# First queries on SP and ScalarE, a third of pair 1's queries loaded alone, one x transposition moved: a BigBird attention and gMLP kernel

## The chip, the cores and the metric

The kernel runs on one core of a Trainium2 chip. The metric is the device time of one execution in microseconds (us), lower is better; the median of three runs of the kernel before is 214.83 us. The engines of the core are called here PE (TensorE, with its weight loads as PEld), DVE (VectorE), ACT (ScalarE), POOL (GpSimd) and SP (SyncE, which here issues DMAs and does nothing else).

## The reference

Batch 4, 8 heads, 768 positions, head dimension 64. First a block-sparse attention, then a gMLP layer over its output. Cut to what matters:

```python
scores = scale * np.matmul(q, k.transpose(0, 1, 3, 2))        # [4, 8, 768, 768]
mask = (|blk_i - blk_j| <= 1) | (blk_i in {0, 23}) | (blk_j in {0, 23})
mask[qb*32:(qb+1)*32, kb*32:(kb+1)*32] = True                 # 3 sampled kb for each of 24 qb
attn = softmax(np.where(mask, scores, -1e9))
x = matmul(attn, v)                                           # -> [4, 768, 512]
h = np.maximum(x @ w_in, 0.0)                                 # 512 -> 1024
u, v = h[..., :512], h[..., 512:]
v_n = (v - mean(v)) / sqrt(var(v) + 1e-6)
gated = u * (einsum('ts,bsd->btd', w_spatial, v_n) + b_spatial[None, :, None])
out = gated @ w_out                                           # [4, 768, 512], float32
```

The same 24 by 24 block mask serves all heads and batches.

## The kernel before, in words

**Pairs and heads.** Two heads make a pair; there are 16 pairs, four to a batch element. For a pair the kernel loads `k`, `q` and `v` in float32 (384 KB each, helper `load`, L103 to L107) into staging tiles `st_k`, `st_q`, `st_v`, of which each name has three buffers. It casts them to bf16 (`cast`, L115 to L134): `k` and `q` go side by side into a tile `nat` with positions on the partitions, `v` goes into `vv`. `nat` is then transposed, so that the head dimension is on the partitions, and copied into `kq`, one row of columns for each head: 768 columns of keys (`K_`) and then 768 of queries (`Q_`). For the first four pairs TensorE does the transpositions (`head` L278 for pair 0, `tr_first` and `tr_rest` L348 and L356 for the others) and VectorE the copies out of PSUM; later pairs are transposed by DMA.

**The mask.** Rows 64 to 87 of `kq` (`MR`) hold the mask: for keys a one-hot of the block, for queries the 24 allowances (0 or -300) of the query's block. The scores matmul contracts over 88 rows and so adds the mask. The key rows are made once for head 0 by iota and compare; the query rows come from three small matmuls (`mask_rows`, L272) whose results are copied by ACT (twice) and DVE (once). `rows` (L239) copies both kinds of rows from head 0 to the other heads, on ACT, POOL or DVE.

**Slots.** The main loop (L807) goes through slots. In slot s, in program order: the scores of the slot (`qk_unit`, four matmuls of 256 columns, or two of 512, L406, then one Exp over 128x1024 on ACT, L411), what is listed in `pre` for the slot, the attention-times-`vv` matmuls that are due (`av_unit`, L452; normalisation by L434 and L435), what is listed in `at` (`when`), some steps of the gMLP products from a queue (`run_queue`, L546), and what is listed in `late`. The first 36 slots treat batch element 0 in units of three slots: `UNITS` 0 and 1 are the two heads of pair 0, units 2, 3, 4 the first third of the queries of pairs 1, 2, 3, and so on. The order is written out by hand and each engine executes its instructions in the order of the program.

The entries that matter here: pair 1's first transpositions (`tr_first(1)`: all keys and the first third of the queries) in slot 4, `tr_first(2)` in slot 7, `tr_first(3)` in slot 10; the rest of the queries of pair 1 (`tr_rest(1)`) in slot 8. `av_unit` of unit 0 begins in slot 5 and needs pair 0's `v`; that of pair 2 begins in slot 12. `xtr_third(u)` transposes a finished third of the attention output `x` for the gMLP; those of units 1 and 2 stand in `late` of slot 13, unit 1's first (L715 and L716).

**Queues.** DMAs are issued by SP one after the other in program order, except for the first keys and first queries of head 0, which ACT issues (L137, L138). SP's order is: sampled blocks, the rest of head 0's and head 1's keys, head 1's queries, then `k1 q1 v0 k2 q2 v1 k3 q3 v2`, the last third of pair 0's queries, `v3`, eight pieces of `w_in`. A load waits on SP for a free staging buffer, and what follows on SP waits with it. Pair 0's queries keep their buffer until their last third has been loaded and cast (L320, L324), so that the load of pair 3's queries has the choice of the two buffers of pairs 1 and 2 alone. POOL makes nearly all of the casts, in the same order as the loads: `k1 q1 v0 k2 q2 v1 k3 q3`, a `rows` copy, `v2 v3`, the last of pair 0's queries, `w_in`.

**Fillers.** `filler(n, to)` issues matmuls of zeros that only keep TensorE busy: 26 at the start, and `FILL2 = (6, 0, 2)` at three places of the setup.

Of the kernel before, what the change touches and what calls it, by code (L numbers as in the profile page):

```python
# [10 lines left out]
FP32 = mybir.dt.float32  # L11
# [6 lines left out]
def _listify(ap: bass.AP) -> bass.AP:  # L18
    t = ap.tensor
    if isinstance(t.shape, tuple):  # L20
        t = dataclasses.replace(t, shape=list(t.shape))
        ap = dataclasses.replace(ap, tensor=t)
    return ap
# [3 lines left out]
def kernel(  # L27
# [16 lines left out]
    nc = tc.nc  # L44

    B, H, S, D = q.shape
# [3 lines left out]
    NCH = S // 128  # L50
# [12 lines left out]
    TC = NCH // NT  # L63
    TW = TC * 128
    S0 = NT * NG * 3
    FILL, FILL2, FILL3 = 26, (6, 0, 2), 4
    U_DVE = (0, 1, 2, 3)

    const = ctx.enter_context(tc.tile_pool(name="const", bufs=1))
# [1 line left out]
    psum = ctx.enter_context(tc.tile_pool(name="psum", bufs=1, space=bass.MemoryType.PSUM))  # L71
# [13 lines left out]
    MR = slice(D, KR)  # L85
    K_, Q_ = slice(0, S), slice(S, 2 * S)

    def qcols(t0, n=1):
        return slice(S + t0 * TW, S + (t0 + n) * TW)
# [4 lines left out]
    def dram(src, p, hs=slice(0, 2), cs=slice(0, NCH)):  # L94
        b, g = divmod(p, NG)
        return src[b, 2 * g + hs.start:2 * g + hs.stop].rearrange(
            "h (p c) d -> p h (c d)", c=NCH)[:, :, cs.start * D:cs.stop * D]

    H0, H1, BOTH = slice(0, 1), slice(1, 2), slice(0, 2)
    ALLC, C01, C03, C45 = slice(0, NCH), slice(0, TC), slice(0, 2 * TC), slice(2 * TC, NCH)  # L100
    SRC = {"k": k, "q": q, "v": v}

    def load(p, nm, hs=BOTH, cs=ALLC, eng=nc.sync):  # L103
        if (nm, p) not in st:
            st[nm, p] = work.tile([128, 2, S // 2], FP32, tag="st_" + nm, bufs=3, name="st_" + nm)
        eng.dma_start(out=st[nm, p][:, hs, cs.start * D:cs.stop * D],  # L106
                      in_=dram(SRC[nm], p, hs, cs))  # L107
# [4 lines left out]
    def nat0_view():  # L112
        return nat[0].rearrange("p c h d -> p (c h d)").rearrange("p (h x) -> p h x", h=2)

    def cast(p, nm, eng, hs=BOTH, cs=ALLC):  # L115
        if nm == "v":
            dst = vv[p % NVV][:, hs, cs, 0:D]
        else:
            if p not in nat:
                nat[p] = work.tile([128, 2 * NCH, 2, D], BF16, tag="nat", bufs=4, name="nat")  # L120
            c0 = 0 if nm == "k" else NCH
            dst = nat[p][:, c0 + cs.start:c0 + cs.stop].rearrange("p c h d -> p h c d")[:, hs]
        src = st[nm, p].rearrange("p h (c d) -> p h c d", d=D)[:, hs, cs]
        if p == 0 and nm != "v":
            dst = nat0_view()[:, hs, (c0 + cs.start) * D:(c0 + cs.stop) * D]
            if cs is not C45:
                dst = dst[:, 0].rearrange("p (i t d) -> p t i d", t=2, d=D)
                src = src[:, 0].rearrange("p (t i) d -> p t i d", t=2)
            else:
                dst = dst.rearrange("p h (c d) -> p h c d", d=D)  # L130
        if eng is nc.scalar:
            nc.scalar.activation(out=dst, in_=src, func=AF.Copy)
        else:
            eng.tensor_copy(out=dst, in_=src)  # L134

    samp = const.tile([KR, 2 * NR], I32)
    load(0, "k", H0, C03, eng=nc.scalar)  # L137
    load(0, "q", H0, C03, eng=nc.scalar)  # L138
    nc.sync.dma_start(out=samp[MR], in_=_listify(sampled_blocks).bitcast(I32))
    load(0, "k", H0, C45)  # L140
    load(0, "k", H1)
    load(0, "q", H1, C03)
    load(1, "k")
    load(1, "q")
    load(0, "v")
    load(2, "k")
    load(2, "q")
    load(1, "v")


# [27 lines left out]
    wps = psum.tile([128, 512], FP32, tag="av", bufs=2)  # L178

    def filler(n, to):  # L180
        for _ in range(n):
            nc.tensor.matmul(out=to[:, 0:128], lhsT=warm, rhs=warm, start=True, stop=True)
# [28 lines left out]
    PL, DV = nc.gpsimd, nc.vector  # L211
# [27 lines left out]
    def rows(hs, cs, eng=nc.vector):  # L239
        src = kq[MR, 0:1, cs].to_broadcast([NB, hs.stop - hs.start, cs.stop - cs.start])  # L240
        if eng is nc.scalar:
            nc.scalar.activation(out=kq[MR, hs, cs], in_=src, func=AF.Copy)
        else:
            eng.tensor_copy(out=kq[MR, hs, cs], in_=src)

    cast(0, "k", nc.scalar, H0, C03)
    rows(H1, K_, nc.scalar)
    rows(slice(2, 3), slice(0, 512), nc.scalar)
    cast(0, "q", PL, H0, C03)
    cast(0, "k", PL, H0, C45)  # L250
    cast(0, "k", PL, H1)
    cast(0, "q", PL, H1, C03)


# [2 lines left out]
    def moe_tag():  # L257
        moe_tags.rotate(1)
        if moe_tags[0] in held:
            moe_tags.rotate(1)  # L260
        return moe_tags[0]

    def bank(nm="ps", tag=None):
        return psum.tile([128, 1024], BF16, tag=tag or moe_tag(), bufs=2 if tag else 1, name=nm)
# [7 lines left out]
    def mask_rows(ps, t0, n, copy, rs=slice(0, KR)):  # L272
        nc.tensor.matmul(out=ps[:, 0:n * TW], lhsT=bm[rs],
                         rhs=kq[rs, 0, t0 * TW:(t0 + n) * TW], start=True, stop=True)
        return lambda: copy(kq[MR, 0, qcols(t0, n)], ps[0:NB, 0:n * TW])


    def head(ps, h, c0, n, at=0):  # L278
        for i in range(0, n, 2):
            nc.tensor.transpose(out=ps[:, at + i * 64:at + (i + 2) * 64],  # L280
                                in_=nat0_view()[:, h, (c0 + i) * D:(c0 + i + 2) * D],
                                identity=ident)

    def split0(ps, h, c0, n, t, copy=dve_copy):
        w = n * 64
        copy(kq[0:D, h, c0 * 128 + t * w:c0 * 128 + (t + 1) * w], ps[t * D:(t + 1) * D, 0:w])

    K4, K2, Q4 = (0, 2 * TC), (2 * TC, NCH - 2 * TC), (NCH, 2 * TC)
    ps0 = bank()
    head(ps0, 0, *K4)  # L290
    split0(ps0, 0, *K4, 0)
    split0(ps0, 0, *K4, 1)
    filler(FILL2[0], wps)
    psq = bank("psq", "av")
    head(psq, 0, *Q4)
    split0(psq, 0, *Q4, 0)
    filler(FILL2[1], wps)
    mask_rows(psum.tile([128, 1024], FP32, tag="sc", bufs=2, name="mq"), 0, 1, act_copy)()
    m1 = mask_rows(psum.tile([128, 512], FP32, tag=moe_tag(), bufs=1, name="mq"), 1, 1, act_copy)
    m2 = mask_rows(psum.tile([128, 1024], FP32, tag="sc", bufs=2, name="mq"), 2, 1, dve_copy, MR)  # L300
    filler(FILL2[2], wps)
    split0(psq, 0, *Q4, 1)
    m1()
    m2()
    rows(H1, qcols(0, NT), PL)
    rows(slice(2, 3), slice(512, S), PL)

    cast(1, "k", PL)
    cast(1, "q", PL)
    cast(0, "v", PL)  # L310
    load(3, "k")
    cast(2, "k", PL)
    cast(2, "q", PL)
    cast(1, "v", PL)
    load(3, "q")
    cast(3, "k", PL)
# [379 lines left out]
    at, late, pre = {}, {}, {}  # L696

    def when(slot, *fns):
        at.setdefault(slot, []).extend(fns)

    def c(f, *a, **kw):
        return lambda: f(*a, **kw)

    K_Q0 = slice(0, S + TW)
    ROWS = [(1, 2, 8, qcols(0)), (1, 3, 4, K_), (5, 4, 6, K_), (6, 6, 8, K_), (14, 4, 8, qcols(1, 2))]
    when(0, second)
    when(1, third)
    when(2, lambda: filler(FILL3, psum.tile([128, 512], FP32, tag=moe_tag(), bufs=1, name="wps")))
    for p, sl in ((1, 4), (2, 7), (3, 10)):
        when(sl, c(tr_first, p))  # L710
    for sl, h0, h1, cs in ROWS:
        when(sl, c(rows, slice(h0, h1), cs))
    for p, sl in ((1, 8), (2, 11), (3, 14), (0, 17)):
        when(sl, c(tr_rest, p, 2 if p == 0 else 1))
    for u in range(1, len(UNITS)):  # L715
        late.setdefault({1: 13, 2: 13}.get(u, 3 * u + 7), []).append(c(xtr_third, u))  # L716

    def moe_begin(b):
        moe[b] = Moe(b)
# [139 lines left out]
```

## Time and profile before

| | |
|---|---|
| median of three runs | 214.83 us (214.56 to 215.42) |
| profiled execution | 215.21 us, of which 213.4 us are the span from the first to the last instruction |
| busy share of the span | PE 97%, PEld 61%, DVE 62%, ACT 80%, POOL 34% |
| first Exp of the scores (slot 0) | starts at 6.02 us |
| the 36 Exps of batch element 0 (L411) | 6.02 to 44.03 us, with 2.4 us of idle time of ACT among them |
| DMA | 41.70 MB, mean 195 GB/s; 306 to 386 GB/s from 6 to 15 us |

Each row of a timeline gives the start, the duration, the engine, the line of the kernel, the operation with its output and input tiles, the number of merged instructions, and in brackets the idle time of the engine before it with what ended that time. Durations and starts are us from the start of the span. The scores of the first slots start on PE at 5.38, 5.94, 7.09, 8.10, 8.93 (slots 0 to 4), 10.93, 12.29, 13.58, 15.10, 16.14 (5 to 9), 16.84, 18.24, 19.18, 20.14 and 21.59 us (10 to 14).

From the DMA view, the landing times of the loads (issue plus time to landing): head 1's queries 5.57, `k1` 7.16, `q1` 9.87, `v0` 10.95, `k2` 12.0, `q2` 13.0, `v1` 14.1, `k3` 15.1, `q3` 16.2, `v2` 17.2, the last third of pair 0's queries 17.6, `v3` 18.7 us.

### The profile page before, as it was taken

The page shows a single profiled execution, that of the slowest core. Times are in us where ns is not written, and L with a number is a line of the kernel's source. Part 1 is how long each engine was busy: PE and PEld are TensorE (multiplying, and loading weights), DVE is VectorE, ACT ScalarE, POOL GpSimd, SP SyncE. Part 2 cuts the span into 40 slices and gives each one's busy share as a digit, 9 for nine tenths or more (in the row PEclk, how much of TensorE's full clock was granted, in tenths as well). Part 3 has the DMA queues.
Part 4 walks back from the last instruction along what each step waited for, and adds up shares of the span by engine and source line. Part 5 has one row for each costly group of instructions (what it writes and reads, how often), then busy time and mean ns, then how long its engine had stood idle before and what let it go on. Part 6 is the DMA issues. An engine that isn't in the chain of part 4 may idle for free.

```text
span 213.4 us, 5299 instructions
## 1 busy us (share of the span) xinstructions
PE 206.6 (97%) x2151; PEld 130.9 (61%) x2151; DVE 131.9 (62%) x287; ACT 171.0 (80%) x226; POOL 72.9 (34%) x119
## 2 busy tenths in 40 slices
PE   8799999999999999999999999999999999999992
PEld 7578887866666665665665565566656656544441
DVE  7589875988854535385887445286784433476551
ACT  6969999999999899979989788978989787266021
POOL 6589669867572405042442040130120000012000
PEclk9969999999999999999999999999999999999999
DMA  5999799999999999999691497697100324610265
GB/s 161 345 342 332 249 316 218 340 191 326 266 375 190 292 191 299 236 280 304 127 259 37 73 289 172 198 307 116 37 3 19 67 52 94 235 55 0 51 172 200
DMA packets 62780, 41.70 MB, mean 195 GB/s; under 512 B 44580, under 2 KB 57508, under 8 KB 62756
## 3 DMA queue, kind: packets, MB, share of 16 engines
q1 hardware_dynamic: 62324, 40.97, 74.7%
q10 hardware_dynamic: 432, 0.39, 0.6%
q8 instruction: 17, 0.28, 0.5%
q14 instruction: 7, 0.06, 0.1%
HBM read 24.38 MB, written 6.29 MB: 144 GB/s over the span
## 4 chain that ended last, share of the span: by engine, by line
PE 92%; DMA 3%; SPq 1%; ACT 1%; POOL 0%; DVE 0%; issue 0%; ACTq 0%
PE ps_moe L546 33%; PE ps L419 22%; PE ps_av L470 13%; PE ps_t L546 7%; PE ps L406 7%; PE ps_av L452 4%; PE ps_sc L546 4%; DMA st_q<-in_q_dram 3%; PE ps L267 1%; SPq L106 1%; PE ps_av L267 1%; ACT osb L217 0%; POOL nat L134 0%; ACT a_all L423 0%; DVE xn L435 0%
## 5 line engine op out<-in xcount | busy, mean ns | idle before, releaser
L423 ACT ACTIVATE a_all<-ps 128x768 bf16<-128x768 f32 x144 | 113.9, 812 | 14.9 <-PE ps L419 7.4
L419 PE MATMUL ps<-kq 88*128 88x384 bf16 x288 | 70.5, 325 | 0.1
L470 PEld LDWEIGHTS <-a_all 128*128 128x128 bf16 x864 | 46.5, 97 | 20.0
L470 PE MATMUL ps_av<-vv,a_all 128*128 128x65 bf16 x864 | 51.2, 194 | 0.0
L419 PEld LDWEIGHTS <-kq 88*128 88x128 bf16 x288 | 28.0, 98 | 31.0 <-issue 0.9
L546 PE MATMUL ps_moe<-w_in_t,xt 128*128 128x512 bf16 x144 | 44.0, 378 | 0.0
L411 ACT ACTIVATE a_all<-ps 128x1024 bf16<-128x1024 f32 x36 | 35.1, 1025 | 3.4 <-PE ps L406 2.9
L546 PE MATMUL ps_moe<-vn,w_spt 128*128 128x512 bf16 x108 | 32.7, 378 | 0.0
L134 POOL CAST nat<-st_k 128x768 bf16<-128x768 f32 (+2 forms) x17 | 13.6, 802 | 41.1 <-DMA st_k<-in_k_dram 40.8
L434 DVE RECIPROCAL rc<-ps_av 128x6 f32<-128x6 f32 (+1 forms) x36 | 6.7, 185 | 28.2 <-PE ps_av L470 26.6
L614 DVE SCALAR_TENSOR_TENSOR un<-ps_moe,b_col,un 128x512 bf16<-128x512 f32 x18 | 13.5, 750 | 16.7 <-PE ps_moe L546 16.1
L406 PE MATMUL ps<-kq 88*128 88x256 bf16 (+1 forms) x140 | 22.9, 286 | 0.7 <-ACT a_all L411 0.7
L583 POOL TENSOR_SCALAR std<-mv 128x3 f32<-128x3 f32 (+1 forms) x9 | 2.1, 238 | 62.2 <-DVE mv L580 45.5
L546 PE MATMUL ps_moe<-w_out_t,gt 128*128 128x512 bf16 x72 | 21.5, 378 | 0.0
L546 PEld LDWEIGHTS <-xt 128*128 128x128 bf16 x192 | 15.4, 97 | 7.2 <-DVE xt L214 0.2
L435 DVE TENSOR_TENSOR xn<-ps_av,rc 128x384 bf16<-128x384 f32 (+1 forms) x36 | 18.5, 513 | 1.2
L579 DVE BATCH_NORM_STATS2 stats<-vn 128x6 f32<-128x512 bf16 x24 | 16.5, 687 | 1.4 <-ACT vn L574 0.9
L134 POOL CAST nat<-st_q 128x768 bf16<-128x768 f32 (+1 forms) x18 | 14.1, 782 | 6.9 <-DMA st_q<-in_q_dram 6.5
L406 PEld LDWEIGHTS <-kq 88*128 88x128 bf16 x140 | 12.8, 100 | 4.6 <-issue 0.8
L134 POOL CAST vv<-st_v 128x768 bf16<-128x768 f32 x16 | 13.6, 855 | 5.7 <-DMA st_v<-in_v_dram 5.6
L452 PEld LDWEIGHTS <-a_all 128*128 128x128 bf16 x288 | 14.2, 100 | 2.0 <-issue 0.7
L214 DVE COPY kq<-tt 64x1536 bf16<-64x1536 bf16 x24 | 15.0, 627 | 0.3
(84 smaller groups left out, 211.8 us busy)
## 6 DMA issues: line engine op xcount, KB each, us to landing
st_v<-in_v_dram SPq DMA_DIRECT2D x16, 384.0 KB, 6.0
out_dram<-osb SPq DMA_DIRECT2D x23, 256.0 KB, 3.1
st_k<-in_k_dram SPq DMA_DIRECT2D x15, 384.0 KB, 4.4
st_q<-in_q_dram SPq DMA_DIRECT2D x15, 384.0 KB, 5.4
ws_f<-in_moe_w_spatial_dram SPq DMA_DIRECT2D x6, 384.0 KB, 6.6
w_f<-in_moe_w_in_dram SPq DMA_DIRECT2D x8, 256.0 KB, 5.9
w_f<-in_moe_w_out_dram SPq DMA_DIRECT2D x4, 256.0 KB, 4.2
st_q<-in_q_dram SPq DMA_DIRECT2D x2, 128.0 KB, 4.7
```

The source lines that it names most:

```text
L134: eng.tensor_copy(out=dst, in_=src)
L214: nc.vector.tensor_copy(out=o, in_=i)
L406: nc.tensor.matmul(out=ps[:, at:at + n * TW], lhsT=kq[:, h, ci * 128:(ci + 1) * 128], rhs=kq[:, h, qcols(t0, n)], start=True, stop=True)
L411: nc.scalar.activation(out=out, in_=ps, func=AF.Exp, scale=0.125)
L419: nc.tensor.matmul(out=ps[:, hf * 512:hf * 512 + HALF], lhsT=kq[:, j % H, ci * 128:(ci + 1) * 128], rhs=kq[:, j % H, S + hf * HALF:S + (hf ...
L423: nc.scalar.activation(out=a_ref["h", j][:, ci, :].rearrange("p (b c) -> p b c", b=2), in_=ps.rearrange("p (b c) -> p b c", b=2)[:, :, 0:H ...
L435: nc.vector.tensor_tensor(out=out, in0=ps[:, :, 0:D], in1=rc[:, 0:n].to_broadcast([128, n, D]), op=ALU.mult)
L452: nc.tensor.matmul(out=av_ref[u][:, to, :], lhsT=a_ref[u][:, at:at + 128], rhs=vv[pp % NVV][:, h, ci, :], start=(ci == 0), stop=(ci == NCH ...
L470: nc.tensor.matmul(out=av_ref[j][:, qc, :], lhsT=a_ref["h", j][:, ci, qc * 128:(qc + 1) * 128], rhs=vv[p % NVV][:, h, ci, :], start=(ci == ...
L546: nc.tensor.matmul(out=ref["ps"][:, 0:w], lhsT=lhs(i), rhs=rhs(i), start=(i == 0), stop=(i == n - 1))
L579: nc.vector.bn_stats(out=stats, in_=self.vn[:, tcc, :])
L614: nc.vector.scalar_tensor_tensor(out=self.un[:, tcc, :], in0=ps, scalar=b_col[:, tcc:tcc + 1], in1=self.un[:, tcc, :], op0=ALU.add, op1=AL ...
```

## The change

It does four things.

1. The first queries of head 0 are issued by SP, behind the sampled blocks, instead of by ACT, and are cast by ACT instead of POOL. ACT's copies of mask rows shrink (head 1's key rows in two halves, the second half behind the two copies of query rows) and head 2's key rows are made by DVE in slot 1 instead of by ACT and POOL. POOL casts head 1's keys before the rest of head 0's.
2. The setup's order changes: the three mask matmuls contract over the 24 mask rows alone, and the copies out of PSUM are in the order keys, queries, keys, queries. Four of the eight fillers of `FILL2` go.
3. Pair 1's queries are loaded and cast in two parts: the first third (`C01`, 128 KB, rows of 512 bytes) at the old place, the other two thirds (`C25`, 256 KB) behind pair 2's queries, on SP and on POOL.
4. `xtr_third(2)` moves from `late` of slot 13 to `pre` of slot 14, which is behind slot 14's scores.

```diff
-    FILL, FILL2, FILL3 = 26, (6, 0, 2), 4
+    FILL, FILL2, FILL3 = 26, (2, 2), 4
...
     load(0, "k", H0, C03, eng=nc.scalar)
-    load(0, "q", H0, C03, eng=nc.scalar)
     nc.sync.dma_start(out=samp[MR], in_=_listify(sampled_blocks).bitcast(I32))
+    load(0, "q", H0, C03)
     load(0, "k", H0, C45)
     load(0, "k", H1)
     load(0, "q", H1, C03)
     load(1, "k")
-    load(1, "q")
+    load(1, "q", cs=C01)
     load(0, "v")
     load(2, "k")
     load(2, "q")
+    load(1, "q", cs=C25)
     load(1, "v")
...
     cast(0, "k", nc.scalar, H0, C03)
-    rows(H1, K_, nc.scalar)
-    rows(slice(2, 3), slice(0, 512), nc.scalar)
-    cast(0, "q", PL, H0, C03)
+    cast(0, "q", nc.scalar, H0, C03)
+    rows(H1, slice(0, 384), nc.scalar)
+    cast(0, "k", PL, H1)
     cast(0, "k", PL, H0, C45)
-    cast(0, "k", PL, H1)
     cast(0, "q", PL, H1, C03)
...
     split0(ps0, 0, *K4, 0)
-    split0(ps0, 0, *K4, 1)
     filler(FILL2[0], wps)
     psq = bank("psq", "av")
     head(psq, 0, *Q4)
+    m0 = mask_rows(psum.tile([128, 1024], FP32, tag="sc", bufs=2, name="mq"), 0, 1, act_copy, MR)
+    m0()
     split0(psq, 0, *Q4, 0)
+    split0(ps0, 0, *K4, 1)
+    m1 = mask_rows(psum.tile([128, 512], FP32, tag=moe_tag(), bufs=1, name="mq"), 1, 1, act_copy, MR)
+    m1()
+    split0(psq, 0, *Q4, 1)
+    m2 = mask_rows(psum.tile([128, 1024], FP32, tag="sc", bufs=2, name="mq"), 2, 1, dve_copy, MR)
     filler(FILL2[1], wps)
-    mask_rows(psum.tile([128, 1024], FP32, tag="sc", bufs=2, name="mq"), 0, 1, act_copy)()
-    m1 = mask_rows(psum.tile([128, 512], FP32, tag=moe_tag(), bufs=1, name="mq"), 1, 1, act_copy)
-    m2 = mask_rows(psum.tile([128, 1024], FP32, tag="sc", bufs=2, name="mq"), 2, 1, dve_copy, MR)
-    filler(FILL2[2], wps)
-    split0(psq, 0, *Q4, 1)
-    m1()
     m2()
+    rows(H1, slice(384, S), nc.scalar)
     rows(H1, qcols(0, NT), PL)
-    rows(slice(2, 3), slice(512, S), PL)
 
     cast(1, "k", PL)
-    cast(1, "q", PL)
+    cast(1, "q", PL, cs=C01)
     cast(0, "v", PL)
     load(3, "k")
     cast(2, "k", PL)
     cast(2, "q", PL)
+    cast(1, "q", PL, cs=C25)
     cast(1, "v", PL)
     load(3, "q")
...
-    ROWS = [(1, 2, 8, qcols(0)), (1, 3, 4, K_), (5, 4, 6, K_), (6, 6, 8, K_), (14, 4, 8, qcols(1, 2))]
+    ROWS = [(1, 2, 8, qcols(0)), (1, 2, 4, K_), (5, 4, 6, K_), (6, 6, 8, K_), (14, 4, 8, qcols(1, 2))]
...
     for u in range(1, len(UNITS)):
-        late.setdefault({1: 13, 2: 13}.get(u, 3 * u + 7), []).append(c(xtr_third, u))
+        where, slot = (pre, 14) if u == 2 else (late, 13 if u == 1 else 3 * u + 7)
+        where.setdefault(slot, []).append(c(xtr_third, u))
```

More of the change, by code (lines that the diff above doesn't have):

```diff
@@ L99 @@
     H0, H1, BOTH = slice(0, 1), slice(1, 2), slice(0, 2)
-    ALLC, C01, C03, C45 = slice(0, NCH), slice(0, TC), slice(0, 2 * TC), slice(2 * TC, NCH)
+    ALLC, C01, C03 = slice(0, NCH), slice(0, TC), slice(0, 2 * TC)
+    C25, C45 = slice(TC, NCH), slice(2 * TC, NCH)
     SRC = {"k": k, "q": q, "v": v}
```

## The prediction

> **What bounds the kernel now.** I began with the page's rows of slices (where engines idle, where the clock falls), then the chain of waits over the first 23 us, the timeline there, and the waits of TensorE. From 21.5 us to the end the waits show none for PE: it is dense, in program order. A microsecond won or lost before 22 us is therefore passed on to the end nearly whole.
>
> The chain that ended last, in order of time (start, duration, what):
>
> ```profile
> 3.04 6.83 DMA st_q<-in_q_dram
> 9.92 0.84 POOL nat L134
> 10.80 0.29 PE ps L267 x2
> 11.09 0.85 PE ps L406 x2
> ...
> 20.98 0.43 DVE xn L435
> 21.42 0.05 issue
> 21.46 0.28 PE ps_av L267 x2
> 21.75 0.44 PE ps L406 x4
> ```
>
> Pair 1's queries are issued at 3.04, land at 9.87 and are cast by 10.75; only then can the last two transpositions of `tr_first(1)` run, and slot 5's scores behind them. Later the chain passes once more through a vector operation: `xtr_third(2)` waits for `xn`, with slot 14's scores queued behind it. The timeline around it, PE and ACT:
>
> ```profile
> 10.80 0.29 PE L267 MATMUL ps<-ident,nat 128*128 128x128 bf16 x2 [0.94 <-POOL nat L134]
> 11.98 1.02 ACT L411 ACTIVATE a_all<-ps 128x1024 bf16<-128x1024 f32 x1 [1.27 <-PE ps L406]
> 21.46 0.28 PE L267 MATMUL ps_av<-ident,xn 128*128 128x128 bf16 x2 [0.25 <-DVE xn L435]
> 22.23 18.74 ACT L411 ACTIVATE a_all<-ps 128x1024 bf16<-128x1024 f32 x19 [0.40 <-PE ps L406]
> ```
>
> Busy time in three stretches (PE first, PEclk behind POOL):
>
> ```profile
> 7.56:10.97 3.41, 2.05 (x22) 1.47 (x21) 1.44 (x5) 3.15 (x4) 1.39 (x2) 1.00 1.05 370
> 10.97:14.39 3.42, 3.42 (x28) 2.26 (x26) 3.19 (x4) 2.05 (x2) 2.82 (x4) 0.50 1.04 354
> ```
>
> A stretch with PE busy 2.05 of 3.41 us is followed by one at half clock; the stretch before it, with 3.09 busy, was not. What the half clock costs: the chain's five pieces of scores and attention of slots 5 to 7 (0.85, 0.53, 0.85, 0.44, 0.79) sum to 3.46, at full clock the same pieces are 0.44, 0.26, 0.44, 0.26, 0.44 = 1.84; so 1.62 us of PE time.
>
> The third view is SP's queue:
>
> ```profile
> 6.18 0.82 SPq L106 DMA_DIRECT2D st_k<-in_k_dram  x1
> 10.77 0.37 SPq L106 DMA_DIRECT2D st_q<-in_q_dram  x1
> ```
>
> `q3` is issued 0.02 us after the cast of `q1` ends (9.92 + 0.83 = 10.75): it waits for a buffer, and `v2`, the rest of pair 0's queries, `v3` and `w_in` wait behind it.
>
> **Part 1 and 2, the setup.** SP gets one more issue (0.43) ahead of everything; ACT loses one (0.46), which only lets its table load start earlier, and then it waits for keys that land at 0.72 + 2.2 = 2.92. The first queries landed at 1.15 + 2.5 = 3.65; from SP, issued at 1.21, I take 3.6. ACT's cast: 0.40, by the row of the keys (128x256, 0.40), so 4.0 against 4.13 on POOL. Then on ACT 0.49 of mask rows (24x384, between the 24x256 copy of 0.37 and the 24x512 copy of 0.61), two copies of 0.37, 0.49 again: 4.0 + 1.72 = 5.72, but the first query-row copy waits for the mask matmul, which waits for `bm` at 4.15 on DVE, and its result is ready about 4.65; so ACT is free at 5.9. DVE has four copies of 0.30 from 4.18; the third ends at 5.2, the scores' end is near 5.85. First Exp 5.9 against 6.02: a gain of 0.1, bounds 0.3 and -0.2 (queries landing up to 0.43 late). POOL loses a copy (0.39) and a cast (0.40); DVE gains 24x768 in slot 1 (0.35 by its own row), under its idle 2.05 us before 11.13, so nothing. Without that cover it would cost 0.35. Fillers: four of them are 0.4 us at the cold clock, under waits. Slots 0 to 4 end on ACT at 10.6 instead of 10.71.
>
> **Part 3, the first third.** In the loaded queue the 128 KB of pair 0's rest landed at 17.6, 0.4 behind `v2` and 1.07 ahead of `v3` (11.70 + 5.9, 11.19 + 6.0, 12.27 + 6.4). 384 KB take 1.05 there, 128 KB 0.41: the third lands 0.64 earlier, at 9.23 (to 9.66 if SP's extra issue shows). The trace has no 512-byte rows of `q1`, so the bounds are 0 and 1.05 earlier; I take 0.64. Its cast is 0.40 (128x256), not 0.83: done at 9.7, against 10.75. PE reaches these transpositions near 9.8, so slot 5's scores start near 10.0 instead of 11.09 and slot 5's Exp loses its 1.27 gap. The next lateness is `v0`: 10.31 + 0.05 + 0.83 = 11.2 against 11.82; PE idles some 0.7 before it. With full clock slot 6's Exp begins at 12.1 (before 13.36), slot 7's at 13.1 (14.60). Then `q2`: lands 12.36, cast to 13.25; slot 8's scores 13.45 (15.26), Exp 14.15 (15.63). The gain here is 1.5 at most; at half clock slots 5 to 7 run as before and slot 8's scores start at 14.7: 0.55. `C25` lands at 13.04 and is cast in 0.61 (the 128x512 casts of `w_in`), 13.9, before `tr_rest(1)` wants it at 14.2.
>
> The rule that speaks against the part: the Trainium skill, page DMA: Bandwidth & Descriptors, section Measured (HBM→SBUF, 128 partitions, SWDGE, issued from GpSimd), advises transfers of a megabyte and gives 0.95 us for 64 KB. By 0.95 the third would land only 0.10 earlier and be cast at 10.2, and the gain in slot 5 would shrink by about 0.4; this trace's 0.41 for 128 KB behind other loads contradicts it for queued transfers, and I use the trace.
>
> **What the split gives back.** Pair 3's queries need a buffer of pairs 1 or 2. The first comes free at `q2`'s cast (13.25) or at `C25`'s (13.9), instead of 10.75: their issue moves 2.5 to 3.1 us. They landed 5.4 us after issue, 1.05 behind `k3`, in a full queue. In a short one, pair 4's `k` (issued at 23.00) took 3.4 and 128 KB took 2.2. So issue plus 3.0 to 3.4, not before 16.17: landing 16.25 to 17.3, cast done at 17.1 to 18.2; I take 17.6, in the middle, against 17.01. `tr_first(3)`'s last two transpositions came at 18.28, so 1.27 of slack was there; now its end is near 17.8 instead of 18.40. Of the 1.5 (or 0.55) won, 0.6 is left, bounds 0.0 and 1.1. `v2`, cast 1.96 after `q3` as now, is at 19.56, wanted at 19.45: 0.1. `w_in` is cast by 21.3, wanted at 22.4: free; its cover gone, that would cost what it is late.
>
> **Part 4.** Slot 14's scores (0.44) fill the time in which PE waited for `xn` (0.25 idle, 0.40 on ACT). Gain 0.4, bounds 0 and 0.44 (the chain's piece).
>
> **Sum.** 0.6 + 0.4 = 1.0, with 0.1 lost at `v2`, 0.9 to 1.0. The setup's 0.1 is swallowed by the wait for `q3`. Against the profiled execution 215.21 (span 213.4 and 1.8 around it): 214.2. The profiled run is 0.38 above the median; 214.83 - 1.0 = 213.8.
>
> **The rivals.** *All of it arrives.* `q3` lands in time, because the loads ahead of it finish sooner: then 1.5 + 0.4 = 1.9, 212.9. For it: 16.17 is set by the queue, which has 2 us of slack to lose. Against: two issues in a row depend on casts. *The half clock stays at 11 to 14 us* and nothing else is late: 0.55 + 0.4, 213.9, the same number by another way. *The clock falls a second time.* Now PE waits in slot 10, from about 16.5 to 17.6 or 18.1, for pair 3's queries; if the busy time of its 3.41 us stretch falls toward 2.05, the next stretch runs at half clock and costs 1.62. It decides when the wait passes about 1.2 us (3.41 - 2.05 = 1.36, less other gaps). Then -1.0 + 1.62 = +0.6, and with `q3` at its late end -0.4 + 1.62 = +1.2: 215.4 to 216.0, slower. Against it: PE is otherwise dense there (3.41 of 3.41). The skill's page TensorE: Matmul & The Clock Gate, section What's actually happening, lets the clock fall only after a whole idle window of 3.4 us; by that this rival would cost nothing, but the rows above show a fall after a stretch that was 2.05 busy, so it stands.
>
> **How the numbers follow.** The measurement can tell about 0.5%, 1.07 us. The forecast (a gain of about 1, with pair 3's queries as the new limit) gets 0.5, and with bounds 0.4 to 1.5 it lies on the edge: 0.22 faster, 0.28 no change. All of it: 0.18, faster. Half clock alone: 0.14, no change. Second fall: 0.18, slower. So 0.40, 0.42, 0.18. The range takes in the whole gain (with the setup's bound 0.2 more: 212.7) and most of the second fall, up to 215.7.
>
> **What would show it.** First Exp near 5.9; `st_q` of pair 1 landing in two, the first near 9.2; no 1.27 gap before slot 5's Exp; an idle POOL or SP until 13.2 or 13.9 and the issue of `q3` then; a wait of PE for `nat` of about 1 us before slot 11; no wait for `xn`; the clock full, or low from 11 to 14. Wrong it would be if `q3` is issued before 12, if the first third lands after 10, or if PE shows a half clock after 17 us.

## The result, and the profile after

The changed kernel has a median of 215.51 us over 22 runs (213.72 to 216.92), the kernel before 214.46 us over 22 runs (213.68 to 215.50): ratio 1.0046, 95% interval 1.0029 to 1.0063. It is slower by 1.0 us; the forecast was a gain of about 1.0 us. A second set of 12 runs gave 1.0029 (1.0006 to 1.0051).

The profiled execution took 216.92 us (span 215.0), the slowest of the 22, so its losses are larger than the typical ones; the kernel before was profiled at 215.21, also above its median. What these two executions say is checked below with more of them.

The chain of waits of the changed kernel (start, duration, what):

```profile
11.75 0.87 POOL nat L135
12.62 0.02 issue
12.64 0.37 SPq L107
13.01 0.05 issue
13.06 6.34 DMA st_v<-in_v_dram
...
19.52 0.83 POOL vv L135
20.36 0.04 issue
20.40 0.42 PE ps_av L454 x8
```

The long wait for pair 1's queries before slot 5 is out of the chain. In its place stands pair 2's `v`: POOL ends the cast of pair 2's queries at 12.62, SP can then issue pair 3's queries, then `v2` at 13.06, and `v2` lands at 19.40. TensorE, in slot 12, waits for it.

The timeline of the same execution, ACT, POOL, SP and PE:

```profile
5.78 7.49 ACT L413 ACTIVATE a_all<-ps 128x1024 bf16<-128x1024 f32 x8
8.57 0.72 POOL L135 CAST nat<-st_q 128x256 bf16<-128x256 f32 x1
12.64 0.37 SPq L107 DMA_DIRECT2D st_q<-in_q_dram  x1
13.06 1.03 SPq L107 DMA_DIRECT2D st_v<-in_v_dram  x1
20.40 0.42 PE L454 MATMUL ps_av<-vv,a_all 128*128 128x65 bf16 x8 [1.93 <-POOL vv L135]
21.29 1.02 ACT L413 ACTIVATE a_all<-ps 128x1024 bf16<-128x1024 f32 x1 [1.95 <-PE ps L408]
```

Eight Exps run without a gap from 5.78, where ACT had gaps of 1.27, 0.36 and 0.21 before: the gain of slots 5 to 7 is there. Then 1.93 us of PE go in slot 12. Two stretches of 3.41 us, PE busy first, the clock behind POOL:

```profile
17.89:21.30 3.41, 1.48 (x31) 1.32 (x29) 1.84 (x5) 1.46 (x3) 1.25 (x2) 1.00 0.86 275
21.30:24.72 3.42, 3.42 (x36) 2.93 (x33) 1.81 (x5) 2.04 (x2) 3.13 (x7) 0.50 0.88 311
```

The wait emptied the first, and the clock was half in the second. The first Exp of the stage after the 36 (L425, L423 before) starts at 45.62 instead of 43.92: 1.70 later, and the profiled time is 1.71 longer. All of the loss lies ahead of 46 us.

### The profile page after: what moved, and what is told of

Read it like the earlier page. It is cut to its first block, busy times and chain, and to the rows that moved or that the text cites. A ratio compares the mean times of both kernels' runs of the same rounds, so it can differ in the third digit from the quotient of the medians.

```text
span 215.0 us, 5292 instructions
## 1 busy us (share of the span) xinstructions
PE 207.0 (96%) x2147; PEld 131.3 (61%) x2147; DVE 131.1 (61%) x287; ACT 171.0 (80%) x227; POOL 74.5 (35%) x118
## 4 chain that ended last, share of the span: by engine, by line
PE 88%; DMA 6%; SPq 2%; POOL 1%; ACT 1%; issue 0%; ACTq 0%; POOLq 0%
PE ps_moe L548 32%; PE ps L421 22%; PE ps_av L472 13%; PE ps_t L548 7%; PE ps L408 5%; PE ps_sc L548 3%; PE ps_av L454 3%; DMA st_q<-in_q_dram 3%; DMA st_v<-in_v_dram 3%; SPq L107 2%; PE ps L268 1%; PE ps_av L268 1%; ACT osb L219 0%; POOL nat L135 0%; POOL vv L135 0%
## 5 line engine op out<-in xcount | busy, mean ns | idle before, releaser
L425 ACT ACTIVATE a_all<-ps 128x768 bf16<-128x768 f32 x144 | 113.9, 813 | 14.9 <-PE ps L421 7.4
L472 PE MATMUL ps_av<-vv,a_all 128*128 128x65 bf16 x864 | 51.2, 194 | 0.0
L454 PE MATMUL ps_av<-vv,a_all 128*128 128x65 bf16 x288 | 15.3, 196 | 2.2 <-POOL vv L135 2.2
L135 POOL CAST vv<-st_v 128x768 bf16<-128x768 f32 x16 | 14.4, 899 | 7.4 <-DMA st_v<-in_v_dram 7.0
L135 POOL CAST nat<-st_q 128x768 bf16<-128x768 f32 (+2 forms) x18 | 14.5, 808 | 3.4 <-DMA st_q<-in_q_dram 3.2
```

The costliest lines, as they stand in the source:

```text
L425: nc.scalar.activation(out=a_ref["h", j][:, ci, :].rearrange("p (b c) -> p b c", b=2), in_=ps.rearrange("p (b c) -> p b c", b=2)[:, :, 0:H ...
L454: nc.tensor.matmul(out=av_ref[u][:, to, :], lhsT=a_ref[u][:, at:at + 128], rhs=vv[pp % NVV][:, h, ci, :], start=(ci == 0), stop=(ci == NCH ...
L472: nc.tensor.matmul(out=av_ref[j][:, qc, :], lhsT=a_ref["h", j][:, ci, qc * 128:(qc + 1) * 128], rhs=vv[p % NVV][:, h, ci, :], start=(ci == ...
```

## The experiments

All ratios are against runs of the kernel before, taken together with them on the same chip. **Theory A**: the split holds pair 1's buffer until the second part is cast, so pair 3's queries are issued late, and all that is behind them on SP is late with them. **Rival B**: the setup's reordering costs the time. **Rival C**: the loss is a half clock that some executions meet.

### Pair 1's queries whole again

```diff
-    load(1, "q", cs=C01)
+    load(1, "q")
-    load(1, "q", cs=C25)
     (the casts likewise)
```

> The changed kernel with pair 1's queries loaded and cast whole again (part 3 undone). Theory A (the split delays pair 3's queries and pair 2's v behind them on SP, and TensorE then waits 1.93 us for pair 2's v in slot 12): pair 3's queries are issued near 10.5 us again, no wait for vv in slot 12, the gap before slot 5's Exp is back; 213.9 to 214.4 us where the kernel before has 214.5. Rival B (the setup's reordering costs the time): still about 215.5 us.

214.09 us, 0.9984 (0.9958 to 1.0011). POOL, SP and ACT:

```profile
8.75 0.96 POOL L135 CAST nat<-st_q 128x768 bf16<-128x768 f32 x1
9.73 0.37 SPq L107 DMA_DIRECT2D st_q<-in_q_dram  x1
10.52 1.02 ACT L411 ACTIVATE a_all<-ps 128x1024 bf16<-128x1024 f32 x1 [0.19 <-PE ps L406]
```

The loss is gone without the split, as A says; the setup is in this kernel, so B alone can't make it. But the expected gap before slot 5's Exp did not come back: 0.19. Pair 1's whole queries were cast from 8.75 here, from 9.92 in the profile of before. So the kernel before may have had less to win than its profile showed.

### The split alone

The kernel before with part 3 only.

```diff
-    load(1, "q")
+    load(1, "q", cs=C01)
...
     load(2, "q")
+    load(1, "q", cs=C25)
     (the casts likewise)
```

> The kernel before with part 3 alone. Theory A: slot 5 starts about 1 us earlier, but PE waits 1 to 2 us for vv in slot 12, as in the changed kernel: 215.0 to 215.9 us. Rival B (the setup costs): the split alone gains, 213.5 to 214.0 us.

215.02 us, 1.0019 (0.9988 to 1.0049): at the lower edge of A, and not told from no change. Its profiled execution took 216.25; the two longest waits of PE behind the start (total, times, longest):

```profile
PE ps_moe L549 <- DVE vn L190: 1.4, 1, 1.4
PE ps_moe L549 <- POOL w_in_t L232: 1.0, 1, 1.0
```

`q3` was issued at 11.86, and this time neither it nor `v2` stopped PE, but a piece of `w_in`, further back in the same queue, at 22.67 us, and a gMLP product behind a vector operation. The latter wait lies at 53.80 us; that the late queue makes it too is not shown.

### Pair 2's v ahead of the waiting load

```diff
     load(3, "k")
+    load(2, "v")
...
-    load(2, "v")
```

> The changed kernel with pair 2's v issued by SP right behind pair 3's k, ahead of the waiting load of pair 3's queries. Theory A: pair 2's v lands by 16 us, the wait of 1.93 us in slot 12 goes, pair 3's queries may cost up to 1 us in slot 10: 213.4 to 214.3 us. Rival C (the loss is the half clock at 21 to 24.6 us by chance, not the late load): still 215.3 to 215.7 us.

215.54 us, 1.0050 (1.0021 to 1.0079): a miss. It is as slow as the changed kernel, though `v2` is issued at 7.40. The number is one that rival C gave, but only two of the 12 runs have a mean clock under 0.995, and the profile, at full clock, shows another cause:

```profile
12.13 0.88 SPq L107 DMA_DIRECT2D st_q<-in_q_dram  x2
18.27 0.28 PE L268 MATMUL ps<-ident,nat 128*128 128x128 bf16 x2 [1.40 <-POOL nat L135]
```

`q3`, issued at 12.13, is cast from 17.39 and PE waits 1.40 for it in slot 10. Moving one victim out of the queue only makes the next one the victim. Theory A as first put (it is `v2` that costs) was too narrow; A2 is: whatever waits behind the buffer is late, and which of it stops PE differs from execution to execution.

### Four staging buffers for queries

```diff
-FP32, tag="st_" + nm, bufs=3,
+FP32, tag="st_" + nm, bufs=4 if nm == "q" else 3,
```

> The changed kernel with four staging buffers for queries instead of three, so that no load waits for a cast. Theory A: pair 3's queries are issued near 7.5 us, pair 2's v right behind, no wait of PE in slots 10 to 14, and the whole gain of slots 5 to 8 and of slot 14 arrives: 212.5 to 213.5 us. Rivals B and C: 215 us or more.

214.13 us, 0.9979 (0.9952 to 1.0006). Once more, with runs of its own of the kernel before:

> The changed kernel with four staging buffers for queries, once more, to narrow its interval: 0.997 to 0.999 of the kernel before, and 0.4 to 0.7% under the changed kernel. If the first result was chance of its runs: 1.000 or above.

214.04 us, 0.9985 (0.9963 to 1.0006). SP in the first of the two:

```profile
7.80 0.87 SPq L107 DMA_DIRECT2D st_q<-in_q_dram  x1
```

Removing the wait alone, with the split and everything else kept, takes off 0.4 to 0.7% (0.9979 and 0.9985 against 1.0046 and 1.0029, each against its own runs of the kernel before). The setup is still in this kernel, so B does not make the loss; nor does C, since of the 22 runs of the changed kernel only the profiled one has a mean clock under 0.996. The whole expected gain (212.5 to 213.5 us) did not come. The second profile shows that a transfer can be late without the wait too: `q3`, issued at 7.49, landed 9.1 us later, 2.4 behind pair 3's keys, where it came 1.0 to 1.1 behind them in the other three profiles with four buffers; PE waited 1.18 us for it.

```profile
16.61 0.83 POOL L135 CAST nat<-st_q 128x768 bf16<-128x768 f32 x1 [1.64 <-DMA st_q<-in_q_dram]
```

### The setup alone

The kernel before with parts 1 and 2 only: the changed kernel with the edit of the first experiment and this one.

```diff
-        where, slot = (pre, 14) if u == 2 else (late, 13 if u == 1 else 3 * u + 7)
-        where.setdefault(slot, []).append(c(xtr_third, u))
+        late.setdefault({1: 13, 2: 13}.get(u, 3 * u + 7), []).append(c(xtr_third, u))
```

> The kernel before with parts 1 and 2 alone (setup and first queries). Theory A2 (the split makes pair 3's queries wait for a buffer on SP until 12 us, and whatever stands behind, queries, v or w_in, then stops TensorE in slots 10 to 16; the other parts cost nothing): 214.0 to 214.6 us where the kernel before has 214.7, first Exp near 5.7 us. Rival B (the setup's reordering costs time): 215 us or more. Rival D (the setup brings pair 1's whole queries from 9.9 to 8.7 us and with it most of the gain in slot 5): 213.7 to 214.2 us and no gap of over 0.5 us before slot 5's Exp.

214.80 us, 1.0024 (0.9997 to 1.0051) against 214.38 for the kernel before: a miss for A2, which allowed 214.6 at most where the kernel before has 214.7, a ratio of 0.9995. The ratio is one that B gave (1.0014 or more), but the interval takes in no change; so there is no gain, and a small cost of the setup stays open. Its profile, with whole queries cast from 9.89, met the half clock at the place where the kernel before had met it:

```profile
8.27:11.69 3.42, 2.06 (x18) 1.24 (x17) 1.84 (x4) 2.58 (x4) 2.00 (x3) 1.00 1.04 372
11.69:15.10 3.41, 3.29 (x36) 2.76 (x35) 2.64 (x5) 2.40 (x3) 2.73 (x5) 0.50 1.02 349
```

Rival D falls with it: the same setup had whole queries at 8.75 in one execution and at 9.89 in this one. A count beside it: of the 48 runs with the new setup and whole queries (this kernel, the one above twice, and the one with four buffers) 7 have a mean clock under 0.993; of 114 with the old setup and whole queries none has, though the profiled execution of the kernel before, not among them, has 0.990. So the setup may bring the half clock more often. Fewer fillers may be the reason; no run tells.

### Part 4 alone

The kernel before with `xtr_third(2)` moved; the last diff the other way round.

> The kernel before with part 4 alone (pair 2's x behind slot 14's scores). If the wait for xn in slot 13 is on the path to the end: 0.25 to 0.45 us less than before, 214.3 to 214.5. If it is made up later: no difference, 214.7. In the profile no PE wait on DVE xn near 21 us. Pair 1's queries land near 9.9 us if the setup's order is what brings them forward (rival D), near 8.7 if it is chance of the execution.

214.05 us, 0.9990 (0.9969 to 1.0011): 0.3 us by the medians, inside the interval. The profile has no wait of PE for `xn`; pair 1's queries, with the setup of before, are cast from 9.04, which again speaks for chance in their landing.

### Whole queries and four buffers

```diff
-    load(1, "q", cs=C01)
+    load(1, "q")
-    load(1, "q", cs=C25)
...
-FP32, tag="st_" + nm, bufs=3,
+FP32, tag="st_" + nm, bufs=4 if nm == "q" else 3,
```

> The changed kernel with pair 1's queries whole (part 3 undone) and four staging buffers for queries, so that pair 3's queries wait for no cast. If the buffer wait to 9.7 us in the kernel with whole queries costs nothing, as its slack in slots 10 to 12 says: the same as without the fourth buffer, 214.1 us (213.9 to 214.3). If every wait for the buffer costs: 213.4 to 213.8 us.

214.33 us, 0.9996 (0.9978 to 1.0014). With whole queries the fourth buffer brings nothing: the wait to 9.7 had its slack.

### The changed kernel again

> The changed kernel as it is, once more, for a second profile beside the others. Theory A2: about 0.4 to 0.5% above the kernel before; SP issues pair 3's queries near 12 us; PE waits 1 to 3 us in all in slots 10 to 16, perhaps for another tile than pair 2's v.

214.85 us, 1.0029 (1.0006 to 1.0051). Its profiled execution took 214.61, with the clock full throughout. PE's waits up to 60 us (the first row, the start, left out, and 0.7 us of waits for Exps):

```profile
PE ps L408 <- DVE kq L216: 0.7, 1, 0.7
...
PE ps_moe L548 <- DVE vn L190: 0.4, 1, 0.4
PE ps L268 <- POOL nat L135: 0.2, 1, 0.2
```

These are 1.3 us, none for `v2`; but the wait for `vn` lies at 51.92 us, far behind slot 16, and the 0.7 for `kq` (at 14.57 us) stand in a kernel without the late load too (the last one below, four buffers and the old setup):

```profile
PE ps L409 <- DVE kq L216: 0.8, 1, 0.8
```

Only the 0.2 for `q3` are left as surely its lateness. So the 1.93 us are not the typical wait, and this profile does not show where the typical loss lies.

### Late queries without the split

The late issue alone: pair 1's queries whole, and an unused tile takes the first free staging buffer, so that pair 3's queries wait for pair 2's cast.

```diff
+    spare = work.tile([128, 2, S // 2], FP32, tag="st_q", bufs=3, name="st_q")
+    nc.gpsimd.memset(spare[0:1, 0, 0:1], 0.0)
     load(3, "q")
```

> The changed kernel with pair 1's queries whole (part 3 undone), and an unused tile that takes the first free staging buffer of queries, so that pair 3's queries wait for pair 2's cast as they do with the split. Theory A2 (what costs is the late issue of pair 3's queries, not the split itself): SP issues them near 12.9 us instead of 9.7 and the time rises by 0.4 to 0.7%, from 214.1 to 215.0 to 215.6 us. If the small loads of the split themselves cost (512-byte rows, one more cast on POOL): it stays at 214.1 us.

216.08 us (9 runs), 1.0075 (1.0040 to 1.0111), against 214.46, 0.9998, for the kernel without the spare tile, taken together with it (below). SP and three stretches:

```profile
13.71 0.37 SPq L107 DMA_DIRECT2D st_q<-in_q_dram  x1
```

```profile
7.44:10.86 3.42, 2.15 (x22) 1.43 (x20) 1.72 (x6) 3.06 (x4) 1.63 (x3) 1.00 1.06 375
10.86:14.27 3.41, 3.31 (x29) 2.32 (x28) 3.17 (x4) 2.05 (x2) 2.82 (x4) 0.50 0.63 221
14.27:17.68 3.41, 3.41 (x36) 3.04 (x35) 2.27 (x5) 2.05 (x2) 2.25 (x5) 0.50 0.85 275
```

The late issue alone costs 1.6 us, with no small loads at all, and the fourth buffer takes the loss from the kernel with the split; the two together show that the late issue makes it. Here `q3` comes later still than in the changed kernel (13.71 against 12.64). The profiled execution (217.01) is one with a half clock, two stretches long, and its own time is no measure of the late issue; seven of the nine runs had a mean clock of 0.995 or more, and their median is still 215.97. In the second stretch the DMA share (last column but one) is 0.63 where it was 1.04 before (10.97 to 14.39): SP issues nothing between 8.3 and 13.71, and the transfers run dry. The loads behind start later by that; but in this one profile, with PE at half clock from 10.86 to 17.68, no wait of PE of 0.2 us or more for `q3`, `v2` or `w_in` stands, so that the way from the late issue to the 1.6 us is inferred and not seen.

### Whole queries once more, and the best version

> The changed kernel with part 3 undone (three buffers), once more: 0.998 to 1.000 of the kernel before. With the split free of its wait (four buffers) and the split left out at the same time, the split itself is worth nothing; were it worth its predicted 0.6 us, this kernel would be 0.3% above the one with four buffers.

214.46 us, 0.9998 (0.9975 to 1.0021). That is 0.13% above the kernel with four buffers taken together with it (0.9985), with intervals that overlap: neither 0.3% nor nothing is shut out.

```diff
 (the kernel before, with the edits of part 3, of part 4, and)
-FP32, tag="st_" + nm, bufs=3,
+FP32, tag="st_" + nm, bufs=4 if nm == "q" else 3,
```

> The kernel before with parts 3 and 4 and four staging buffers for queries, that is the changed kernel with four buffers and without parts 1 and 2. If the setup (parts 1 and 2) neither costs nor gains: the same as with it, 0.997 to 0.999 of the kernel before. If it costs (rival B): 0.994 to 0.997. If it gains its 0.1 to 0.2 us: 0.999 to 1.000.

213.68 us, 0.9967 (0.9949 to 0.9985): parts 3 and 4 and the fourth buffer on the old setup. It is the only version that is faster than the kernel before by more than its interval, by 0.7 us as the ratio has it. ACT and SP:

```profile
6.01 8.45 ACT L414 ACTIVATE a_all<-ps 128x1024 bf16<-128x1024 f32 x9 [0.49 <-PE ps L409]
15.37 23.69 ACT L414 ACTIVATE a_all<-ps 128x1024 bf16<-128x1024 f32 x24 [0.91 <-PE ps L409]
```

```profile
7.40 0.62 SPq L107 DMA_DIRECT2D st_q<-in_q_dram  x1
```

33 Exps with one gap of 0.91, where PE waits for a copy of `kq` by DVE. Against the new setup (0.9979, 0.9985) the intervals overlap, and 0.9967 lies at the edge between what a setup without effect (0.997 to 0.999) and one that costs (0.994 to 0.997) would give; that the setup costs is not shown, nor that it doesn't. Nor is the split's own worth: 0.9967 to 0.9985 with it, 0.9996 without it, all with four buffers, overlapping. Both comparisons would need more runs taken together; three kernels meant for that gave no result.

## Why the prediction was wrong

**The setup** went in the profile about as said, first Exp at 5.78 (said 5.9), the queries of head 0 landing at 3.33 (said 3.6); but its 0.1 shows in no time of the runs, and alone it has 1.0024.

**The first third.** Landing at 8.04 (said 9.23), 0.38 behind pair 1's `k`; the 0.41 taken from the queue for 128 KB was right, but it was taken from a landing that was late by itself: in the profile of before `q1` landed 2.71 behind `k1` (9.87 and 7.16), while the loads behind it came 1.0 to 1.1 apart. The 0.95 us that the Trainium skill (page DMA: Bandwidth & Descriptors, section Measured (HBM→SBUF, 128 partitions, SWDGE, issued from GpSimd)) gives for a 64 KB transfer are not what a queued one of 128 KB adds here. Its cast took 0.72 (said 0.40) and began at 8.57, behind that of `k1`. Slot 8's Exp began at 13.43 (15.63 before, said 14.15).

**The step that failed first is the baseline.** The sum took the 1.5 us won in slots 5 to 8, or what `q3` leaves of them (17.8 instead of 18.40), from a profile with a half clock behind slot 5; by the prediction's own figures 0.95 of the 1.5 come from losing that half clock (0.55 where it stays). That the execution stood 0.38 above the median was taken off as a constant. Its clock:

```profile
core 0: 213.4 us, clock 0.990
```

Of 102 further runs of the kernel before, none has a mean clock under 0.995, and 3.41 us at half clock make 0.992. So the median does not pay it. In seven profiles with whole queries these were cast from 8.75, 9.03, 9.04, 9.44, 9.64, 9.89 and 9.92 us; the half clock behind slot 5 is in the last three alone. With the split the cast starts at 8.17 to 8.57 in all seven profiles, and none of them has it. So the split steadies slot 5, but what it takes off the median, once the buffer is there, is by the ratios 0.2 to 0.4 us (0.9979 and 0.9985 against 0.9996, intervals that overlap), not 1.5.

**The term that turned the gain into a loss is what the split gives back, and it was mis-sized.** The mechanism was named: `q3` waits for a buffer, the first of the two bounds (issue at `q2`'s cast, 12.64) was the right one. Its landing was even better than said (15.64, said 16.25 to 17.3). But the loss was put at 0.9 for `q3`, 0.1 for `v2` and nothing for `w_in`. Measured: 1.93 for `v2` in one execution, 1.40 for `q3` in another kernel, 1.0 for `w_in` in a third; over the runs the wait costs 0.9 to 1.4 us (0.4 to 0.7%), and the late issue without the split 1.6. The cast of `v2` was taken to end 1.96 behind that of `q3`; in the profiled execution it ended 3.85 behind, because `v2`, issued 0.42 behind `q3`, landed 3.76 behind it. Why that transfer was so late, and through which waits the typical run loses its 0.9 to 1.4, is not settled.

**The rivals.** The second fall of the clock happened in the profiled execution as described, after a wait in slot 12 instead of slot 10. It was the only one of the 22 runs with a clock of 0.992; it does not carry the median. That the median, 215.51, lies where this rival put the time (215.4 to 216.0) is chance: the other runs lose it without that half clock. *All of it arrives* needed the fourth buffer, and even then it is 0.3 to 0.7 us by the ratios (0.9985 to 0.9967), not 1.9.

**Part 4** did what was said: no wait for `xn` in any profile of a kernel with it (the split alone, without part 4, shows none either). 0.3 us by the medians (0.4 said), not separable from none by itself.

## What to carry to other kernels

Splitting a load in two also lengthens the life of its staging buffer: look for the next load that needs that buffer, and for all that stands behind it on the issuing queue, not only for that load. Moving the one victim ahead only made the next one wait; another buffer took the loss away. The cost need not show as a wait in any one profile. A single profile of a kernel with noisy transfers is one draw: before a stall of it is entered in a sum, check by the clock or the spread of the runs whether the median pays it.

## What the runs showed of the hardware

Pair 1's whole queries landed 1.1 us behind pair 1's keys, issued just before them, in three profiles and 2.1 to 2.7 behind them in four (start of the cast 8.75 to 9.92). Two executions of one and the same kernel had them at 8.7 and 9.4. In the second profile with four buffers `q3` landed 2.4 behind the keys of its pair, and in the changed kernel `v2` landed 3.76 behind `q3`: single loads of the queue came 1 to 3 us late in some executions and not in others. No run tells why.

The clock fell to half after stretches with PE busy 1.48, 2.05, 2.06 and 2.15 of 3.41 us, each time for one or two stretches of 3.41; after a stretch of 2.16 (four buffers, second profile, 13.93 to 17.34) and of 2.35 (whole queries once more, 8.12 to 11.54) it stayed full. Nor does a busy stretch at half clock settle the return: after 3.31 busy (late queries without the split) the next stretch was at half clock again, after 3.29 (the setup alone) at full. The Trainium skill, page TensorE: Matmul & The Clock Gate, section What's actually happening, lets it fall after an idle window; here a stretch with PE busy for three fifths was enough. Counted back from the falls above in steps of 3.41, the stretches begin at another point of the kernel in each execution (10.86 - 6.83 = 4.03 us in one, 11.69 - 6.83 = 4.86 in another), as that section says of free-running windows, so whether a given wait of PE brings the half clock is partly chance.
